# Linear attention mixed with an MLP: the head's loads rearranged, and W4's last 64 features of four chunks multiplied in row halves

## The chip, the cores and the metric

The kernel runs on one core of a Trainium2 chip. The metric is device time in microseconds (us) of one execution. Five engines work side by side, each with its own instruction stream: TensorE (PE in the profile; PEld is its weight loads) multiplies, VectorE (DVE) and ScalarE (ACT) do elementwise work and empty PSUM, GpSimd (POOL) does small setups, and SyncE (SP) mostly issues transfers (DMA). Transfers are also issued by ACT and POOL.

## The reference, cut to what matters

2048 rows of x with 640 features, 32 heads of 20, everything in bfloat16:

```
g = sigmoid((x * gate_w).sum(-1, keepdims=True))

# a: linear attention
q, k, v = split(x @ wqkv);  phi(t) = where(t > 0, t + 1, exp(t)) + 1e-6
num = phi(q) @ (phi(k)^T @ v);  den = phi(q) @ sum(phi(k))
a = (num / (den + 1e-6)) @ wo

# b: mixer and MLP
h  = gelu(layernorm(x) @ w1);  x1 = x + shift4(h) @ w2
b  = x1 + gelu(layernorm(x1) @ w3) @ w4        # w4 is 1728 x 640

out = g * a + (1 - g) * b
```

1728 features are 13 blocks of 128 and a rest of 64.

## The kernel before, in words

The rows are cut into 16 chunks of 128 (c), four of which make a tile of 512 (t). The order on each engine is that of the code; nothing is moved by a scheduler. PSUM is used as four pairs of banks: `pair()` returns the next free one, and a unit that takes a pair waits until the one that had it has been emptied.

The stages, in order: k for all 16 chunks (`k_mm`, L199; `k_evac` empties it), q (`q_unit`, L246), G = x^T phi(k) (`g_unit`, L347), w1 of the MLP (L377), the attention matrices (`kv_unit` L396, `m_unit` L415), w2 (L452), and then for each tile w3 (L499, its 64 rest features at L504) with the next tile's w2 and the attention output (L483) between, and w4 (`w4_unit`, L524).

The k stage multiplies x^T by wk. `wk_sb` has 640 columns of wk and one more, the gate vector, so that the right half of each product (321 columns) also gives x . gate_w. The matmul wants x transposed (`xT`). For chunks 0 to 2 x is loaded in rows and turned by TensorE into PSUM (`x_turn`, L215), from where DVE copies it (L216). For chunks 3 to 15 a transposing transfer brings it straight from memory (L124). wk comes in five pieces of 128 rows (`dc` 0 to 4), all issued by ACT (L129). The gate column is a POOL transfer that scatters 640 single values (L152). `warmup` (L210) multiplies zeros, to keep TensorE busy. The k matmuls of the first three chunks are interleaved by hand as their pieces land (L222 to L233); from chunk 3 on they go chunk by chunk.

SP's queue holds, in order: x chunks 0, 1, 2, the four transposing transfers, wq, the rest of x, and the other weights. wq is re-ordered by five POOL copies (L179) before q uses it. The transfers that SP and ACT issue use eight semaphores in turn, and an issue waits until the last transfer on its semaphore has landed.

In W4 each chunk has two halves of 320 output columns, each a sum over 14 matmuls: 13 blocks of 128 features, and one for the rest of 64. The rest's gelu output h2 holds chunks 0 and 1 on the upper 64 partitions and chunks 2 and 3 on the lower. So there are two copies of the rest's w4 rows, the other 64 partitions of which POOL sets to zero (L432, L433), and the fourteenth matmul runs over all 128 rows. DVE then computes the output chunk `oc` from PSUM (L530), and SP stores it. The last chunk goes in two halves (L526), each stored by itself.

Of the kernel before, what the change touches and what calls it, by code (L numbers as in the profile page):

```python
# [16 lines left out]
def kernel(  # L17
# [25 lines left out]
    FR = F - FF * P
# [12 lines left out]
    out2 = out.rearrange("b s d -> (b s) d")  # L56
# [27 lines left out]
    r_bf = const.tile([P, TS], BF16)  # L84
    ident = const.tile([P, P], BF16)
    ones32 = const.tile([P, 32], BF16)
    wz = const.tile([P, TS], BF16)
    mhalf = const.tile([P, CPT], F32)
    hmask = const.tile([P, H], F32)
    zbd = const.tile([P, DC, H], BF16)  # L90
# [5 lines left out]
    gate = const.tile([P, NCH], F32)  # L96
    omg = const.tile([P, NCH], F32)
# [20 lines left out]
    sp, aq, gq = nc.sync, nc.scalar, nc.gpsimd  # L118

    def load_x(c0, c1):  # L120
        sp.dma_start(x_sb[:, c0:c1, :], x2[c0 * P:c1 * P, :].rearrange("(c p) d -> p c d", p=P))

    def load_xT(c0, c1):
        sp.dma_start_transpose(xT[:, :, c0 * P:c1 * P], x2[c0 * P:c1 * P, :])  # L124

    NPE = 3
    load_x(0, 1)
    for dc in range(DC):
        aq.dma_start(wk_sb[:, dc, 0:D], A_wqkv[dc * P:(dc + 1) * P, D:2 * D])  # L129
    load_x(1, 2)  # L130
    load_x(2, 3)
    load_xT(3, 4)
    load_xT(4, 8)
    load_xT(8, 12)
    load_xT(12, 16)
    sp.dma_start(wq_raw, wqkv_v[:, :, 0:D])
    load_x(3, 8)
    load_x(8, 12)
    load_x(12, 16)
    sp.dma_start(wv_sb[:], wqkv_v[:, :, 2 * D:3 * D])  # L140
# [18 lines left out]
    nc.gpsimd.affine_select(out=hmask[:], in_=hmask[:], compare_op=ALU.is_ge, fill=0.0,
                            base=0, pattern=[[-4, H]], channel_multiplier=1)  # L160
# [25 lines left out]
    def phi(dst, src, n):  # L186
        e = e_p.tile([P, 1024], BF16, name="e")
        ev = e[:, 0:n]
        if len(src.shape) == 3:
            ev = ev.rearrange("p (h e) -> p h e", h=src.shape[1])  # L190
        nc.scalar.activation(ev, src, ACT.Exp)  # L191
        nc.vector.tensor_scalar(e[:, 0:n], e[:, 0:n], 1.0, 1e-6, op0=ALU.min, op1=ALU.add)  # L192
        nc.vector.scalar_tensor_tensor(dst, src, 0.0, ev, op0=ALU.max, op1=ALU.add)

    def k_mm(pt, c, dcs):
        for dc in dcs:
            for hf in range(2):
                n = HD + hf
                nc.tensor.matmul(pt[:, hf, 0:n], lhsT=xT[:, dc, c * P:(c + 1) * P],  # L199
                                 rhs=wk_sb[:, dc, hf * HD:hf * HD + n], start=(dc == 0), stop=(dc == DC - 1))  # L200

    def k_evac(pt, c):
        nc.scalar.copy(ylog[:, c:c + 1], pt[:, 1, HD:HD + 1])
        phi(pk[:, c, :].rearrange("p (h e) -> p h e", h=2), pt[:, :, 0:HD], D)

    warm = pair()

    def warmup(n, w=TS):
        for i in range(n):
            nc.tensor.matmul(warm[:, 1, 0:w], lhsT=wz[:, 0:P], rhs=wz[:, 0:w], start=True, stop=True)  # L210

    def x_turn(c):
        ptb = warm[:, 0, :].bitcast(BF16)
        for dc in range(DC):
            nc.tensor.transpose(ptb[:, dc * P:(dc + 1) * P], x_sb[:, c, dc * P:(dc + 1) * P], ident[:])  # L215
        nc.vector.tensor_copy(xT[:, :, c * P:(c + 1) * P], ptb[:, 0:D].rearrange("p (c s) -> p c s", c=DC))  # L216

    warmup(5)
    kp = [pair() for _ in range(3)]
    x_turn(0)  # L220
    warmup(5, P)
    k_mm(kp[0], 0, (0,))  # L222
    x_turn(1)
    k_mm(kp[0], 0, (1,))
    warmup(2, P)
    x_turn(2)
    k_mm(kp[1], 1, (0, 1))
    k_mm(kp[0], 0, (2,))
    k_mm(kp[1], 1, (2,))
    k_mm(kp[2], 2, (0, 1, 2))  # L230
    for dc in (3, 4):
        for c in range(3):
            k_mm(kp[c], c, (dc,))  # L233
    for c in range(3):
        k_evac(kp[c], c)
    for c in range(3, NCH):
# [191 lines left out]
        ln1_apply(3 * CPT + cc)  # L428
    s1.close()
    w4p = ctx.enter_context(tc.tile_pool(name="w4p", bufs=1))  # L430
    w4_sb = w4p.tile([P, FF + 2, D], BF16)
    nc.gpsimd.memset(w4_sb[FR:P, FF, :], 0.0)  # L432
    nc.gpsimd.memset(w4_sb[0:FR, FF + 1, :], 0.0)  # L433
    nc.gpsimd.dma_start(w4_sb[:, 0:FF, :], B_w4[0:FF * P, :].rearrange("(c p) f -> p c f", p=P))
    nc.gpsimd.dma_start(w4_sb[0:FR, FF, :], B_w4[FF * P:F, :])
    nc.gpsimd.dma_start(w4_sb[FR:P, FF + 1, :], B_w4[FF * P:F, :])
    h2p = ctx.enter_context(tc.tile_pool(name="h2p", bufs=1))
    x1p = ctx.enter_context(tc.tile_pool(name="x1p", bufs=8))
    st = {}
# [5 lines left out]
    def w2_unit(t, cc):  # L445
        c = t * CPT + cc
        if cc == 0:
            st[t] = dict(x1=[], mv=small.tile([P, CPT, 2], F32, name="mv2"))
        pt = pair()
        for hf in range(2):  # L450
            for fc in range(DC):
                nc.tensor.matmul(pt[:, hf, 0:HD], lhsT=hsT[:, fc, 2 + c * P:2 + (c + 1) * P],  # L452
                                 rhs=w2_sb[:, fc, hf * HD:(hf + 1) * HD], start=(fc == 0), stop=(fc == DC - 1))
        x1 = x1p.tile([P, D], F32, name="x1")
        nc.vector.tensor_tensor(x1[:].rearrange("p (h e) -> p h e", h=2), pt[:, :, 0:HD],  # L455
                                x_sb[:, c, :].rearrange("p (h e) -> p h e", h=2), op=ALU.add)
        ln_stats(st[t]["mv"][:, cc, :], x1[:], small.tile([P, 2, 6], F32, name="bnst")[:])
        st[t]["x1"].append(x1)
# [14 lines left out]
    def x1_scale(t, cc):  # L473
        c = t * CPT + cc
        x1 = st[t]["x1"][cc]
        nc.scalar.activation(x1[:], x1[:], ACT.Copy, scale=omg[:, c:c + 1])
# [30 lines left out]
        nc.scalar.activation(h2[:, 2 * i * TS:2 * i * TS + n], pt[:].rearrange("p h e -> p (h e)")[:, 0:n],  # L507
                             ACT.Gelu_apprx_tanh)

    def w4_unit(t, cc):  # L510
        c = t * CPT + cc
        h2, x1 = st[t]["h2"], st[t]["x1"][cc]
        last = c == NCH - 1
        oc = outp.tile([P, D], BF16, name="oc")
        pts = [pair(), pair()] if last else [pair()] * 2
        for hf in range(2):
            hs = slice(hf * HD, (hf + 1) * HD)
            for fc in range(FF + 1):
                if fc < FF:
                    w, l = w4_sb[:, fc, hs], h2[:, fc * TS + cc * P:fc * TS + (cc + 1) * P]  # L520
                else:
                    v, o = cc // 2, FF * TS + (cc % 2) * P
                    w, l = w4_sb[:, FF + v, hs], h2[:, o:o + P]
                nc.tensor.matmul(pts[hf][:, hf, 0:HD], lhsT=l, rhs=w, start=(fc == 0), stop=(fc == FF))  # L524
            if last:
                nc.vector.scalar_tensor_tensor(oc[:, hs], pts[hf][:, hf, 0:HD], omg[:, c:c + 1], x1[:, hs],  # L526
                                               op0=ALU.mult, op1=ALU.add)
                nc.sync.dma_start(out2[c * P:(c + 1) * P, hs], oc[:, hs])
        if not last:
# [21 lines left out]
    for t in range(NT):  # L551
        for i in range(NW3):
            w3_unit(t, i)
            if i < CPT and t + 1 < NT:
                w2_unit(t + 1, i)
            if 2 <= i < 2 + CPT:
                att_unit(t, i - 2)
        if t + 1 < NT:
            ln2_rstd(t + 1, 0, CPT)
            for cc in range(CPT):  # L560
                ln2_apply(t + 1, cc)
        for cc in range(CPT):
            if t + 1 < NT:
                x1_scale(t + 1, cc)
            w4_unit(t, cc)


# [28 lines left out]
```

## Time and profile before

| | us |
|---|---|
| median of 9 runs | 275.02 |
| lowest and highest | 274.70, 275.41 |
| profiled execution | 275.02 |
| its span, first to last instruction | 273.3 |
| TensorE busy | 264.5 (97%) |
| VectorE busy | 141.0 (52%) |
| ScalarE busy | 84.5 (31%) |
| GpSimd busy | 29.2 (11%) |

The span is what the engines' instructions cover; 1.7 us of the execution lie around it. A busy TensorE is not a TensorE at its peak, since matmuls overlap and each one's record lasts longer than its share of the time. Records of the form `L199 PE MATMUL out<-in` name the code line, the engine, the tile written and the tiles read.

### The profile page before, as it was taken

How to read it: one execution, taken by the hardware profiler on the slowest of the kernel's cores; microseconds unless marked ns; L12 is line 12 of the kernel's file. 1: busy time of each engine (PE TensorE's matmuls, PEld its weight loads, DVE VectorE, ACT ScalarE, POOL GpSimd, SP SyncE). 2: the span in 40 equal slices, each digit the busy share in tenths (PEclk: the TensorE clock that was granted, in tenths of full speed). 3: DMA queues.
4: the chain of work that ended last, by engine and by line, in shares of the span. 5: the costliest groups of instructions: out<-in, count | busy, mean ns of one | idle time of the engine just before them, and what ended most of it. 6: DMA issues, size and time to landing. Idle time of an engine off the chain costs nothing.

```text
span 273.3 us, 4333 instructions
## 1 busy us (share of the span) xinstructions
PE 264.5 (97%) x1764; PEld 161.0 (59%) x1781; DVE 141.0 (52%) x275; ACT 84.5 (31%) x124; POOL 29.2 (11%) x65
## 2 busy tenths in 40 slices
PE   5899999999999999999999999999999999999994
PEld 2567644456665564555577555577565577555673
DVE  1169865999994988556242256242256332112212
ACT  1065535531145715831250121250121250232100
POOL 7303100001227223000100000100000000000000
PEclk9999999999999999999999999999999999999999
DMA  7999984100474895000041100051100071100011
GB/s 176 229 240 369 337 269 173 26 2 0 82 110 99 266 170 95 3 0 2 0 94 53 48 0 2 0 100 46 48 2 0 1 93 53 48 2 0 0 50 48
DMA packets 41380, 22.82 MB, mean 83 GB/s; under 512 B 32080, under 2 KB 40272, under 8 KB 41360
## 3 DMA queue, kind: packets, MB, share of 16 engines
q1 hardware_dynamic: 40112, 19.42, 29.5%
q0 software_dynamic: 528, 2.30, 2.6%
q10 hardware_dynamic: 720, 0.82, 1.0%
q8 instruction: 14, 0.23, 0.4%
q14 instruction: 6, 0.05, 0.1%
HBM read 12.21 MB, written 2.62 MB: 54 GB/s over the span
## 4 chain that ended last, share of the span: by engine, by line
PE 94%; DMA 2%; ACT 1%; issue 1%; DVE 0%; ACTq 0%; POOLq 0%
PE pp L524 22%; PE pp L499 20%; PE pp L347 8%; PE pp L452 8%; PE pp L483 8%; PE pp L377 8%; PE pp L246 8%; PE pp L199 8%; DMA wk_sb<-in_gate_w_dram 2%; PE pp L415 1%; PE pp L504 1%; ACT e L191 1%; PE pp L262 0%; PE pp L285 0%; PE pp L215 0%
## 5 line engine op out<-in xcount | busy, mean ns | idle before, releaser
L524 PE MATMUL pp<-w_sb,h 128*128 128x320 bf16 x448 | 61.5, 299 | 0.0
L499 PE MATMUL pp<-lnxT,w_sb 128*128 128x512 bf16 x249 | 59.8, 379 | 0.6
L507 ACT ACTIVATE h<-pp 128x1024 bf16<-128x1024 f32 (+1 forms) x28 | 27.8, 993 | 103.8 <-PE pp L499 95.5
L524 PEld LDWEIGHTS <-h 128*128 128x128 bf16 x448 | 43.5, 98 | 17.5 <-issue 0.8
L499 PEld LDWEIGHTS <-w_sb 128*128 128x128 bf16 x260 | 25.4, 98 | 26.7
L530 DVE SCALAR_TENSOR_TENSOR oc<-pp,omg,x 128x640 bf16<-128x640 f32 x15 | 13.3, 884 | 44.7 <-PE pp L524 44.7
L486 DVE SCALAR_TENSOR_TENSOR x<-pp,gate,x 128x640 f32<-128x640 f32 x16 | 13.9, 868 | 29.4 <-PE pp L483 29.4
L199 PE MATMUL pp<-wk_sb,xT 128*128 128x320 bf16 (+1 forms) x160 | 24.8, 317 | 1.9 <-DMA wk_sb<-in_gate_w_dram 1.6
L455 DVE TENSOR_TENSOR x<-pp,x_sb 128x640 f32<-128x640 f32 x16 | 13.1, 820 | 23.4 <-PE pp L452 23.4
L483 PE MATMUL pp<-m_sb,pqT 128*128 128x320 bf16 x160 | 24.3, 299 | 0.0
L191 ACT ACTIVATE e<-pp 128x640 bf16<-128x640 f32 (+1 forms) x26 | 21.2, 830 | 9.3 <-PE pp L246 9.3
L452 PE MATMUL pp<-w_sb,hsT 128*128 128x320 bf16 x160 | 23.9, 299 | 0.0
L347 PE MATMUL pp<-pk,x_sb 128*128 128x320 bf16 x160 | 22.2, 299 | 0.0
L246 PE MATMUL pp<-xT,wq_sb 128*128 128x512 bf16 x97 | 21.8, 379 | 0.2
L199 PEld LDWEIGHTS <-xT 128*128 128x128 bf16 x160 | 16.4, 103 | 7.4 <-issue 0.6
L318 POOL TENSOR_SCALAR rstd<-mv 128x4 f32<-128x4 f32 (+1 forms) x11 | 3.5, 320 | 158.4 <-DVE mv L324 158.4
L452 PEld LDWEIGHTS <-hsT 128*128 128x128 bf16 x160 | 15.6, 98 | 8.2 <-issue 0.3
L483 PEld LDWEIGHTS <-pqT 128*128 128x128 bf16 x160 | 15.7, 98 | 7.7
L347 PEld LDWEIGHTS <-x_sb 128*128 128x128 bf16 x160 | 15.5, 98 | 6.7 <-issue 0.7
L377 PE MATMUL pp<-lnxT,w_sb 128*128 128x512 bf16 x77 | 17.8, 379 | 0.7 <-ACT hsT L381 0.5
L246 PEld LDWEIGHTS <-wq_sb 128*128 128x128 bf16 x100 | 9.7, 98 | 11.7 <-issue 0.3
L192 DVE TENSOR_SCALAR e<-e 128x640 bf16<-128x640 bf16 (+1 forms) x26 | 9.6, 368 | 9.1 <-ACT e L191 8.6
(84 smaller groups left out, 204.0 us busy)
## 6 DMA issues: line engine op xcount, KB each, us to landing
out_dram<-oc SPq DMA_DIRECT2D x15, 160.0 KB, 1.8
w_sb<-in_B_w_dram SPq DMA_DIRECT2D x1, 2160.0 KB, 9.4
w_sb<-in_B_w_dram POOLq DMA_DIRECT2D x1, 2080.0 KB, 10.8
x_sb<-in_A_x_dram SPq DMA_DIRECT2D x2, 640.0 KB, 10.0
wo_sb<-in_A_wo_dram SPq DMA_DIRECT2D x6, 160.0 KB, 7.6
wk_sb<-in_A_wqkv_dram ACTq DMA_DIRECT2D x5, 160.0 KB, 5.9
hsT<-in_A_wqkv_dram SPq DMA_DIRECT2D x1, 800.0 KB, 5.3
x_sb<-in_A_x_dram SPq DMA_DIRECT2D x1, 800.0 KB, 6.9
```

The lines of the kernel that those rows point to most:

```text
L191: nc.scalar.activation(ev, src, ACT.Exp)
L199: nc.tensor.matmul(pt[:, hf, 0:n], lhsT=xT[:, dc, c * P:(c + 1) * P], rhs=wk_sb[:, dc, hf * HD:hf * HD + n], start=(dc == 0), stop=(dc == ...
L246: nc.tensor.matmul(pt[:, t % 2, :], lhsT=wq_sb[:, dc, j * P:(j + 1) * P], rhs=xT[:, dc, t * TS:(t + 1) * TS], start=(dc == 0), stop=(dc == ...
L347: nc.tensor.matmul(pt[:, hf, 0:HD], lhsT=x_sb[:, c, fc * P:(fc + 1) * P], rhs=pk[:, c, hf * HD:(hf + 1) * HD], start=(c == 0), stop=(c == ...
L377: nc.tensor.matmul(pt[:, i, :], lhsT=w, rhs=lnxT[t][:, dc, :], start=(dc == 0), stop=(dc == DC - 1))
L452: nc.tensor.matmul(pt[:, hf, 0:HD], lhsT=hsT[:, fc, 2 + c * P:2 + (c + 1) * P], rhs=w2_sb[:, fc, hf * HD:(hf + 1) * HD], start=(fc == 0), ...
L483: nc.tensor.matmul(pt[:, hf, 0:HD], lhsT=pqT[:, j, c * P:(c + 1) * P], rhs=m_sb[:, j, hf * HD:(hf + 1) * HD], start=(j == 0), stop=(j == D ...
L486: nc.vector.scalar_tensor_tensor(x1, pt[:, :, 0:HD], gate[:, c:c + 1], x1, op0=ALU.mult, op1=ALU.add)
L499: nc.tensor.matmul(pt[:, k, :], lhsT=w3_sb[:, dc, fc * P:(fc + 1) * P], rhs=lnT[:, dc, :], start=(dc == 0), stop=(dc == DC - 1))
L507: nc.scalar.activation(h2[:, 2 * i * TS:2 * i * TS + n], pt[:].rearrange("p h e -> p (h e)")[:, 0:n], ACT.Gelu_apprx_tanh)
L524: nc.tensor.matmul(pts[hf][:, hf, 0:HD], lhsT=l, rhs=w, start=(fc == 0), stop=(fc == FF))
L530: nc.vector.scalar_tensor_tensor(oc[:].rearrange("p (h e) -> p h e", h=2), pts[0][:, :, 0:HD], omg[:, c:c + 1], x1[:].rearrange("p (h e) - ...
```

## The change

In the head, wk's pieces are issued by ACT (0, 2, 4) and SP (1, 3) in turn. The gate vector is loaded as five rows of 128 (`g5`), turned by TensorE, and copied by DVE into `wk_sb`'s last column. Only x chunk 0 is turned by TensorE, in two parts with a PSUM pair each; chunks 1 to 15 come by seven transposing transfers, chunks 1, 2 and 3 singly, 4 to 7 by twos, 8 to 15 by fours. Chunk 0's k matmuls go in the order 0, 2, 1, 4, 3 of the pieces, the left half first. The warm-up multiplies a constant of ones instead of a tile of zeros that DVE set.

In W4 the tile's four chunks are done together: chunks 0 and 2 first, 13 blocks each; then the rests of all four chunks (`w4_rest`), each over its own 64 partitions and not over 128; then chunks 1 and 3, 13 blocks each. The rest's sums end chunks 0 and 2 and begin chunks 1 and 3. The second copy of the rest's weights lies on the lower 64 partitions of the first, and the zeroing is gone. In the last tile, chunk 3's left half goes ahead of chunk 1, and its right half ends the kernel.

```diff
-    load_x(0, 1)
-    for dc in range(DC):
-        aq.dma_start(wk_sb[:, dc, 0:D], A_wqkv[dc * P:(dc + 1) * P, D:2 * D])
-    load_x(1, 2)
-    load_x(2, 3)
-    load_xT(3, 4)
-    load_xT(4, 8)
-    load_xT(8, 12)
-    load_xT(12, 16)
+    load_x(0, 1)
+    load_wk(aq, 0)
+    load_wk(aq, 2)
+    load_wk(sp, 1)
+    sp.dma_start(g5[:], gate_w.rearrange("(c p) -> c p", p=P))
+    load_wk(aq, 4)
+    load_wk(sp, 3)
+    for c0, c1 in ((1, 2), (2, 3), (3, 4), (4, 6), (6, 8), (8, 12), (12, 16)):
+        load_xT(c0, c1)
     sp.dma_start(wq_raw, wqkv_v[:, :, 0:D])
-    load_x(3, 8)
+    load_x(1, 8)
...
-    with nc.allow_non_contiguous_dma(reason="gate column"):
-        gq.dma_start(wk_sb[:, :, D:D + 1], gate_w.rearrange("(c p o) -> p c o", p=P, o=1))
...
+    warmup(6)
+    kp = pair()
+    turns = [(pair()[:, 0, :].bitcast(BF16), a, b) for a, b in ((0, 2), (2, DC))]
+    tg = warm[:, 0, :].bitcast(BF16)
+    for n, (ptb, a, b) in enumerate(turns):
+        for dc in range(a, b):
+            nc.tensor.transpose(ptb[:, (dc - a) * P:(dc - a + 1) * P], x_sb[:, 0, dc * P:(dc + 1) * P], ident[:])
+        nc.vector.tensor_copy(xT[:, a:b, 0:P], ptb[:, 0:(b - a) * P].rearrange("p (c s) -> p c s", c=b - a))
     warmup(2, P)
...
+    order = (0, 2, 1, 4, 3)
+    k_mm(kp, 0, order[:3], (0,), order[4])
+    nc.tensor.transpose(tg[:, 0:DC], g5[:], ident[0:DC, 0:DC])
+    nc.vector.tensor_copy(wk_sb[:, :, D], tg[:, 0:DC])
+    k_mm(kp, 0, order[3:4], (0,), order[4])
+    k_mm(kp, 0, order[:4], (1,), order[4])
+    k_mm(kp, 0, order[4:], last=order[4])
+    k_evac(kp, 0)
+    for c in range(1, NCH):
...
-    w4_sb = w4p.tile([P, FF + 2, D], BF16)
-    nc.gpsimd.memset(w4_sb[FR:P, FF, :], 0.0)
-    nc.gpsimd.memset(w4_sb[0:FR, FF + 1, :], 0.0)
+    w4_sb = w4p.tile([P, FF + 1, D], BF16)
...
+    def w4_rest(t, ptss, start):
+        for u in range(2):
+            for hf in range(2):
+                for v in range(2):
+                    rows = slice(FR * v, FR * (v + 1))
+                    pts = ptss[u + 2 * v]
+                    if pts is not None:
+                        nc.tensor.matmul(pts[hf][:, hf, 0:HD], lhsT=st[t]["h2"][rows, FF * TS + u * P:FF * TS + (u + 1) * P],
+                                         rhs=w4_sb[rows, FF, hf * HD:(hf + 1) * HD], start=u == 1, stop=u == 0)
...
+    def w4_tile(t):
+        last = t == NT - 1
+        pts = {cc: [pair()] * 2 for cc in (0, 2)}
+        for cc in (0, 2):
+            if t + 1 < NT:
+                x1_scale(t + 1, cc)
+            for hf in range(2):
+                w4_mm(t, cc, pts[cc], hf, True)
+        for cc in (1, 3):
+            pts[cc] = [pair()] * 2
+        w4_rest(t, pts, True)
+        for cc in (0, 2):
+            w4_out(t, cc, pts[cc], (0, 1))
+        for cc, hf in ((3, 0), (1, 0), (1, 1), (3, 1)) if last else ((1, 0), (1, 1), (3, 0), (3, 1)):
+            if t + 1 < NT and hf == 0:
+                x1_scale(t + 1, cc)
+            w4_mm(t, cc, pts[cc], hf, False)
+            if last and cc == 3:
+                w4_out(t, cc, pts[cc], (hf,))
+            elif hf == 1:
+                w4_out(t, cc, pts[cc], (0, 1))
```

What this moves shows at three places. The first is SP's queue at the start, before (DMAHW0 to 7 are the eight semaphores; the code lines are each kernel's own):

```order
L121 DMA x_sb<-in_A_x_dram 128x640 x3
L124 DMA_TRANSPOSE xT<-in_A_x_dram 128x5x128
L124 DMA_TRANSPOSE xT<-in_A_x_dram 128x5x512 [waits DMAHW1_49]
L124 DMA_TRANSPOSE xT<-in_A_x_dram 128x5x512 [waits DMAHW2_49]
L124 DMA_TRANSPOSE xT<-in_A_x_dram 128x5x512 [waits DMAHW3_49]
L136 DMA hsT<-in_A_wqkv_dram 128x5x640 [waits DMAHW4_49]
```

And now (`hsT` holds wq for a while, and `g` is `g5`):

```order
L121 DMA x_sb<-in_A_x_dram 128x640
L127 DMA wk_sb<-in_A_wqkv_dram 128x640
L133 DMA g_89<-in_gate_w_dram 5x128
L127 DMA wk_sb<-in_A_wqkv_dram 128x640
L124 DMA_TRANSPOSE xT<-in_A_x_dram 128x5x128
L124 DMA_TRANSPOSE xT<-in_A_x_dram 128x5x128 [waits DMAHW0_49]
L124 DMA_TRANSPOSE xT<-in_A_x_dram 128x5x128 [waits DMAHW1_49]
L124 DMA_TRANSPOSE xT<-in_A_x_dram 128x5x256 [waits DMAHW2_49]
L124 DMA_TRANSPOSE xT<-in_A_x_dram 128x5x256 [waits DMAHW3_49]
L124 DMA_TRANSPOSE xT<-in_A_x_dram 128x5x512 [waits DMAHW4_49]
L124 DMA_TRANSPOSE xT<-in_A_x_dram 128x5x512 [waits DMAHW5_49]
L138 DMA hsT<-in_A_wqkv_dram 128x5x640 [waits DMAHW6_49]
```

Three transposing transfers more stand ahead of wq, and two wk pieces and the gate ahead of the first of them.

The second place is TensorE at its first k matmuls, before (DMASW0 is the gate column's transfer):

```order
L210 MATMUL pp<-wz 128x128
L199 LDWEIGHTS xT
L199 MATMUL pp<-wk_sb,xT 128x320 [waits DMAHW0_49]
L199 LDWEIGHTS xT
L199 MATMUL pp<-wk_sb,xT 128x321 [waits DMASW0_49]
L215 LDWEIGHTS x_sb [waits DMAHW3_49]
L215 MATMUL pp<-ident,x_sb 128x128
```

And now:

```order
L198 LDWEIGHTS xT [waits DVE_49]
L198 MATMUL pp<-wk_sb,xT 128x320 [waits DMAHW2_49]
L198 LDWEIGHTS xT
L198 MATMUL pp<-wk_sb,xT 128x320 [waits DMAHW3_49]
L223 LDWEIGHTS g_89 [waits DMAHW5_49]
L223 MATMUL pp<-ident,g_89 128x5
L198 LDWEIGHTS xT
L198 MATMUL pp<-wk_sb,xT 128x320 [waits DMAHW4_49]
L198 LDWEIGHTS xT
L198 MATMUL pp<-wk_sb,xT 128x321 [waits DVE_49]
```

The second k matmul used to wait for the scattered column; now the gate's turn follows three left halves, and the first right half waits for DVE's copy of it.

The third place is TensorE in W4. Before, in the first tile, where one chunk ends and the next begins (the numbers tell the PSUM pairs apart):

```order
L524 LDWEIGHTS h2_1376
L524 MATMUL pp_1601<-w4_sb_1101,h2_1376 128x320
L524 LDWEIGHTS h2_1376
L524 MATMUL pp_1634<-w4_sb_1101,h2_1376 128x320 [waits PE_49]
L524 LDWEIGHTS h2_1376
L524 MATMUL pp_1634<-w4_sb_1101,h2_1376 128x320
```

And now, in the second tile, where chunk 2's blocks end and the rests run:

```order
L503 LDWEIGHTS h2_1718
L503 MATMUL pp_1942<-w4_sb_1090,h2_1718 128x320
L514 LDWEIGHTS h2_1718
L514 MATMUL pp_1941<-w4_sb_1090,h2_1718 128x320
L514 LDWEIGHTS h2_1718
L514 MATMUL pp_1942<-w4_sb_1090,h2_1718 128x320
L514 LDWEIGHTS h2_1718
L514 MATMUL pp_1941<-w4_sb_1090,h2_1718 128x320
L514 LDWEIGHTS h2_1718
L514 MATMUL pp_1942<-w4_sb_1090,h2_1718 128x320
L514 LDWEIGHTS h2_1718
L514 MATMUL pp_1997<-w4_sb_1090,h2_1718 128x320 [waits DVE_49]
```

One pair at a time was filled; now neighbouring matmuls go to two pairs by turns.

More of the change, by code (lines that the diff above doesn't have):

```diff
@@ L86 @@
     ones32 = const.tile([P, 32], BF16)
-    wz = const.tile([P, TS], BF16)
+    g5 = const.tile([DC, P], BF16)
     mhalf = const.tile([P, CPT], F32)
@@ L124, in load_xT, with load_wk @@
         sp.dma_start_transpose(xT[:, :, c0 * P:c1 * P], x2[c0 * P:c1 * P, :])
-    NPE = 3
+    def load_wk(q, dc):
+        q.dma_start(wk_sb[:, dc, 0:D], A_wqkv[dc * P:(dc + 1) * P, D:2 * D])
     load_x(0, 1)
-    for dc in range(DC):
-        aq.dma_start(wk_sb[:, dc, 0:D], A_wqkv[dc * P:(dc + 1) * P, D:2 * D])
-    load_x(1, 2)
-    load_x(2, 3)
-    load_xT(3, 4)
-    load_xT(4, 8)
-    load_xT(8, 12)
-    load_xT(12, 16)
+    load_wk(aq, 0)
[6 more added lines that the diff above has]
+        load_xT(c0, c1)
     sp.dma_start(wq_raw, wqkv_v[:, :, 0:D])
-    load_x(3, 8)
+    load_x(1, 8)
     load_x(8, 12)
@@ L147 @@
     sp.dma_start(w3_sb[:], B_w3.rearrange("(c p) f -> p c f", p=P))
-    nc.vector.memset(wz[:].bitcast(U32), 0)
-    with nc.allow_non_contiguous_dma(reason="gate column"):
-        gq.dma_start(wk_sb[:, :, D:D + 1], gate_w.rearrange("(c p o) -> p c o", p=P, o=1))
+    nc.gpsimd.memset(mhalf[:], -0.5)
     nc.gpsimd.memset(ident[:], 1.0)
@@ L156 @@
     nc.vector.memset(ones32[:], 1.0)
-    nc.gpsimd.memset(mhalf[:], -0.5)
     nc.gpsimd.memset(hmask[:], 1.0)
@@ L193, in phi, with k_mm @@
         nc.vector.scalar_tensor_tensor(dst, src, 0.0, ev, op0=ALU.max, op1=ALU.add)
-    def k_mm(pt, c, dcs):
+    def k_mm(pt, c, dcs, hfs=(0, 1), last=DC - 1):
         for dc in dcs:
-            for hf in range(2):
+            for hf in hfs:
                 n = HD + hf
                 nc.tensor.matmul(pt[:, hf, 0:n], lhsT=xT[:, dc, c * P:(c + 1) * P],
-                                 rhs=wk_sb[:, dc, hf * HD:hf * HD + n], start=(dc == 0), stop=(dc == DC - 1))
+                                 rhs=wk_sb[:, dc, hf * HD:hf * HD + n], start=(dc == 0), stop=(dc == last))
     def k_evac(pt, c):
@@ L206 @@
     warm = pair()
+    one = nc.const_aps.tensor(1.0, (P, TS), BF16)
     def warmup(n, w=TS):
         for i in range(n):
[L210 to L224, printed above, removed]
-    warmup(2, P)
[L226 to L236, printed above, removed]
+            nc.tensor.matmul(warm[:, 1, 0:w], lhsT=one[:, 0:P], rhs=one[:, 0:w], start=True, stop=True)
+    warmup(6)
[6 more added lines that the diff above has]
+        nc.vector.tensor_copy(xT[:, a:b, 0:P], ptb[:, 0:(b - a) * P].rearrange("p (c s) -> p c s", c=b - a))
+    warmup(2, P)
+    order = (0, 2, 1, 4, 3)
[7 more added lines that the diff above has]
+    for c in range(1, NCH):
         pt = pair()
@@ L430 @@
     w4p = ctx.enter_context(tc.tile_pool(name="w4p", bufs=1))
-    w4_sb = w4p.tile([P, FF + 2, D], BF16)
-    nc.gpsimd.memset(w4_sb[FR:P, FF, :], 0.0)
-    nc.gpsimd.memset(w4_sb[0:FR, FF + 1, :], 0.0)
+    w4_sb = w4p.tile([P, FF + 1, D], BF16)
     nc.gpsimd.dma_start(w4_sb[:, 0:FF, :], B_w4[0:FF * P, :].rearrange("(c p) f -> p c f", p=P))
     nc.gpsimd.dma_start(w4_sb[0:FR, FF, :], B_w4[FF * P:F, :])
-    nc.gpsimd.dma_start(w4_sb[FR:P, FF + 1, :], B_w4[FF * P:F, :])
+    nc.gpsimd.dma_start(w4_sb[FR:P, FF, :], B_w4[FF * P:F, :])
     h2p = ctx.enter_context(tc.tile_pool(name="h2p", bufs=1))
@@ L508, in w3_unit, with w4_mm, w4_out @@
                              ACT.Gelu_apprx_tanh)
-    def w4_unit(t, cc):
-        c = t * CPT + cc
[L512 to L529, printed above, removed]
+    def w4_mm(t, cc, pts, hf, start):
+        for fc in range(FF):
+            nc.tensor.matmul(pts[hf][:, hf, 0:HD], lhsT=st[t]["h2"][:, fc * TS + cc * P:fc * TS + (cc + 1) * P],
+                             rhs=w4_sb[:, fc, hf * HD:(hf + 1) * HD], start=start and fc == 0,
+                             stop=not start and fc == FF - 1)
+    def w4_rest(t, ptss, start):
[7 more added lines that the diff above has]
+                                         rhs=w4_sb[rows, FF, hf * HD:(hf + 1) * HD], start=u == 1, stop=u == 0)
+    def w4_out(t, cc, pts, hfs):
+        c = t * CPT + cc
+        x1 = st[t]["x1"][cc]
+        oc = oc_of.setdefault(c, None) or outp.tile([P, D], BF16, name="oc")
+        oc_of[c] = oc
+        if len(hfs) == 2:
             nc.vector.scalar_tensor_tensor(oc[:].rearrange("p (h e) -> p h e", h=2), pts[0][:, :, 0:HD],
@@ L533, in w4_unit @@
             nc.sync.dma_start(out2[c * P:(c + 1) * P, :], oc[:])
+        else:
+            hf = hfs[0]
+            hs = slice(hf * HD, (hf + 1) * HD)
+            nc.vector.scalar_tensor_tensor(oc[:, hs], pts[hf][:, hf, 0:HD], omg[:, c:c + 1], x1[:, hs],
+                                           op0=ALU.mult, op1=ALU.add)
+            nc.sync.dma_start(out2[c * P:(c + 1) * P, hs], oc[:, hs])
+    oc_of = {}
+    def w4_tile(t):
[19 more added lines that the diff above has]
+                w4_out(t, cc, pts[cc], (0, 1))
     for cc in range(CPT):
@@ L561 @@
                 ln2_apply(t + 1, cc)
[L562 to L565, printed above, removed]
+        w4_tile(t)
 _INS = ['A_x', 'A_wqkv', 'A_wo', 'B_x', 'B_w1', 'B_w2', 'B_w3', 'B_w4', 'gate_w']
```

## The prediction

> **What bounds the kernel now.** I read the page first, for which engine carries the span, then the chain that ended last, then the first 25 us in order of time with the landings of their transfers, since half of the change lies there.
>
> ```profile
> span 273.3 us, 4333 instructions
> PE 264.5 (97%) x1764; PEld 161.0 (59%) x1781; DVE 141.0 (52%) x275; ACT 84.5 (31%) x124; POOL 29.2 (11%) x65
> PE 94%; DMA 2%; ACT 1%; issue 1%; DVE 0%; ACTq 0%; POOLq 0%
> 1.32 6.25 DMA wk_sb<-in_gate_w_dram
> ...
> 9.15 0.37 PE pp L210 x2
> 9.53 0.53 PE pp L215 x5
> 10.06 4.57 PE pp L199 x22
> ...
> 16.86 16.51 PE pp L199 x120
> 33.37 0.22 PE pp L246
> ...
> 37.69 1.20 PE pp L262 x32
> ...
> 74.95 0.33 PE pp L297 x4
> ...
> 85.12 0.78 PE pp L396 x15
> ...
> 92.62 2.83 PE pp L415 x80
> ...
> 115.30 2.16 PE pp L499 x10
> ...
> 136.67 0.67 PE pp L504 x10
> 137.34 15.32 PE pp L524 x112
> ```
>
> Rows of the chain are start, length, what ran, how often. TensorE carries 94% of it, and from 33.37 us on it hardly waits. So a gain is either a TensorE stream made shorter, or the k stage (L199) ending before 33.37. The change does one of each: W4 is four streams like the 15.32 us row, and the head holds the one long wait, for the gate vector.
>
> The k stage has 160 matmuls (16 chunks of 10). The row at 16.86 gives 16.51/120 = 0.1376 us each, so 22.0 us would do; it ends at 33.37. The missing 11.4 us are a late start, waits, and a low pace: 22 matmuls took 4.57 us. Two stretches of L199 show the pace; in brackets stands how many records touch a stretch.
>
> ```profile
> 10.10:13.10 3.00, 3.00 (x13) 1.00 1.28 257
> 17.00:33.00 16.00, 16.00 (x119) 1.00 1.04 345
> L199 PE MATMUL pp<-wk_sb,xT x160: 296/300/475, 5.6 to 33.1; 128*128 128x320 bf16 x80, 128*128 128x321 bf16 x80
> ```
>
> The slowest record lasts 0.475 us, so 13 records touching 3.00 us start (3.00 + 0.475)/13 = 0.267 us apart, about half the later pace (the clock column reads 1.00 in both and does not show it). With n at the wide spacing among the 22, 0.267n + 0.1376(22 - n) = 4.57 gives n = 12: the pace doubles at about 13.2 us, 4.1 us after TensorE last began to work without a gap (9.15).
>
> **The head, step by step.** These rows are the head's first turn and TensorE's two waits after it, the issues, the landings (us from the issue's start), and POOL's group that copies wq.
>
> ```profile
> 3.79 0.71 PE L215 MATMUL pp<-ident,x_sb 128*128 128x128 bf16 x5 [0.23 <-DMA x_sb<-in_A_x_dram]
> 4.54 0.49 DVE L216 COPY xT<-pp 128x640 bf16<-128x640 bf16 x1 [3.31 <-PE pp L215]
> 5.09 0.69 PE L210 MATMUL pp<-wz 128*128 128x128 bf16 x5 [0.58 <-DVE xT L216]
> 7.61 0.43 PE L199 MATMUL pp<-wk_sb,xT 128*128 128x321 bf16 x1 [1.56 <-DMA wk_sb<-in_gate_w_dram]
> 0.80 1.34 SPq L121 DMA_DIRECT2D x_sb<-in_A_x_dram  x3
> 2.19 1.29 SPq L124 DMA_TRANSPOSE xT<-in_A_x_dram  x1
> 3.76 5.02 SPq L124 DMA_TRANSPOSE xT<-in_A_x_dram  x1
> 12.26 3.32 SPq L124 DMA_TRANSPOSE xT<-in_A_x_dram  x1
> 15.62 0.58 SPq L136 DMA_DIRECT2D hsT<-in_A_wqkv_dram  x1
> xT<-in_A_x_dram SPq DMA_TRANSPOSE x1, 6.4
> xT<-in_A_x_dram SPq DMA_TRANSPOSE x1, 8.3
> xT<-in_A_x_dram SPq DMA_TRANSPOSE x1, 5.3
> hsT<-in_A_wqkv_dram SPq DMA_DIRECT2D x1, 800.0 KB, 5.3
> L179 POOL COPY wq_sb<-hsT 128x320 uint32<-128x320 uint32 x5 | 2.3, 509 | 11.5 <-DMA hsT<-in_A_wqkv_dram 11.5
> wk_sb<-in_A_wqkv_dram ACTq DMA_DIRECT2D x1, 160.0 KB, 6.9
> 2.50:5.00 2.50, 1.77 (x8) 0.71 (x7) 0.46 (x1) 0.64 (x1) 2.03 (x11) 1.00 1.04 360
> 5.00:7.50 2.50, 0.96 (x6) 0.64 (x6) 0.04 (x1) 0.64 (x1) 2.07 (x8) 1.00 0.99 122
> ```
>
> The last column of a stretch is GB/s: 360 until 5.0 us, then 122 while the gate column (landing at 1.32 + 6.25 = 7.57) is under way. wk's last piece was issued at 3.99 and landed 6.9 later, at 10.9.
>
> *wk and x chunk 0.* The x chunk is still SP's first load, so its turn still starts at 3.79. Now x chunk 0 and five wk pieces, 6 x 160 KB, are all issued ahead of anything else: from 2.5 us at 360 GB/s they are through at 5.2, some 0.5 later in place. ACT's fifth issue, which stood back to 3.99, is gone, and so is the gate column; its five rows ride on SP between two pieces. Two turns (2 x 0.14) and the copy of 256 of 640 columns (0.2 to 0.3 of the 0.49) let the first k matmul start at 4.5. A 0.2 us wait for the second copy and 0.4 for the gate's turn and copy (DVE is idle there), and ten matmuls at 0.267, end chunk 0 at 7.6.
>
> *x chunk 1 by DMA transpose.* SP now issues four plain loads first, at 0.45 each (1.34/3), so the first transpose is issued from 2.6 to 3.9. The three landings are at 8.6, 12.1 and 17.6, which is 5.1, 3.3 and 2.0 after the end of their issue. So chunk 1 lands between 5.9 and 9.0. I take 7.5, nearest to the middle row: the 5.1 was spent in the stretch beside the gate column, which is gone. TensorE then goes on at 7.6 without a gap; at 9.0 it would stand for 1.4 us.
>
> *The later chunks.* One chunk's issue is 1.29 and four chunks' 3.32, thus 0.6 plus 0.68 a chunk. Seven issues for 15 chunks take 14.5 us with gaps and end at 17.5; chunks 8 to 11 end theirs at 14.1 and land at 16.1 to 17.4. The k stage needs chunk 8 eight chunks before its end, at 18.3 by the sum below. wq goes out behind them at 17.6, lands 5.3 later at 22.9, and POOL's five copies (0.5 each) end at 25.5, before it is wanted. x_sb, wv, w1 and w3 shift back by some 2 us too, behind stages that begin after 56 us.
>
> *The pace.* Work without a gap begins at 4.5, but for the gate's turn, so 5.6 at the latest if chunk 1 is in time. With the 4.1 us of above the pace doubles at 8.6 to 9.7; I take 9.7. Until then (9.7 - 4.5 - 0.6)/0.267 = 17 matmuls are done, and the other 143 take 19.7: the k stage ends at 29.4 instead of 33.4. **Gain 4.0 us**, and 4.7 with 8.6 (14 before it, end 28.7). What follows is chained to TensorE and moves up with it.
>
> The Trainium skill (TensorE: Matmul & The Clock Gate, Part 1: The HAM clock gate) says that the array gets half its clock until it has been busy for about one free-running window of 3.4 us. The trace agrees: the pace doubles 4.1 us after gapless work starts. Worked out from that page (an estimate), the doubling would come between one and two windows after the start, and a gap would put it off by a whole window; this is the first rival's mechanism.
>
> **W4, step by step.** Before, a tile has 4 chunks x 2 halves x 14 matmuls = 112 in 15.32 us, 0.137 each. The fourteenth multiplies 64 live rows and 64 zero rows. After, 104 full matmuls and 8 on 64 rows each, in pairs on the upper and lower rows with outputs in different pairs of banks. If a pair runs side by side, it costs one. The nearest rows say so: four 32-row matmuls of 512 columns (L297) took 0.33 us, where one full one of 512 takes 2.16/10 = 0.216. Blocks that split the columns do the same: L262 32 in 1.20 (eight fours at 0.1376 would be 1.10), L415 80 in 2.83 (2.75), L504 ten of 256 columns in 0.67 (five at 0.108: 0.54). Each such block pays 0.08 to 0.13 on top, whatever its length; I take 0.11. So 8 x 0.137 = 1.09 becomes 4 x 0.137 + 0.11 = 0.66: 0.43 saved a tile, **1.7 us in all four**. The bounds are 2.2 (no cost on top) and -0.4 (no overlap, 4 x 0.11 more). Weights can't bind: L396 loads a full 128x128 set for each 0.052 us matmul, and a pair needs two in 0.137.
>
> The Trainium skill (TensorEngine Tiling (Array Packing), Key Properties) has a rule against the change: going to another tiling mode drains the array. The 0.08 to 0.13 per block would be that, and it is in the sum.
>
> The rest costs nothing here. The evacuations of chunks 0 and 2 fall in the middle of a tile, where DVE only waits; all four PSUM pairs are held, but the next tile takes them in the same order, and chunk 3's alone comes free last, four units before it is wanted. POOL loses two memsets near 87 us, off the chain. The tail is again 320 columns on DVE and an 80 KB store; chunk 1's full store is issued ahead of it while thirteen matmuls (1.8 us) run, so I add nothing.
>
> **Sum.** The profiled execution took 275.02 us, 1.7 more than its span, and is the median itself. 275.02 - 4.0 - 1.7 = **269.3**.
>
> **Rivals.**
> 1. *The pace doubles late.* Chunk 1 lands at 9.0 or the gaps count against it; gapless work starts at 8.6, the pace doubles at 12.7. Then (12.7 - 4.5 - 1.6)/0.267 = 25 matmuls before it, end 31.3, gain 2.1: 271.2. For it speaks that the kernel before, with gaps of 0.58 and 1.56 us, stayed at the low pace to 13.2; against it, that chunk 1's price of 5.1 has a cause that is removed. 0.24.
> 2. *The transposes set the pace.* If all are issued at the 5.02/4 = 1.25 us a chunk of the second issue, chunks 8 to 11 end theirs at 16.4, land at 19.7, and 80 matmuls later it is 30.7: gain 2.7, time 270.6. For it: that issue stood while ordinary loads ran. Against it: the later ones took 3.3. 0.17.
> 3. *The W4 pairs don't overlap* and only pay the 0.11: 275.02 - 4.0 + 0.4 = 271.4. L297 speaks against it; no row has 64-row strips. 0.08.
> 4. *Slower:* each of the 32 half-row matmuls waits for the one before to leave the array, at the 0.299 us that one lasts from start to end:
>
> ```profile
> L524 PE MATMUL pp<-w_sb,h 128*128 128x320 bf16 x448 | 61.5, 299 | 0.0
> ```
>
> That adds 32 x (0.299 - 0.137) = 5.2, more than the head gives: 276.2. It decides once a half-row matmul costs over 0.26 us (0.137 + 4.0/32). L297's four in 0.33 speak against it. 0.04.
>
> **Chances and range.** My forecast 0.45, the rivals 0.24, 0.17, 0.08, 0.04; two of the first three together, near 273, 0.02. The forecast's own range is 268.1 (4.7 and 2.2) to 270.2. All cases but the slower one and the pairs of rivals lie from 268.1 to 271.4; with 0.4 for the spread of the runs shown (274.7 to 275.41) and for a half-way gap, 268.0 to 272.0. Below 0.2% (0.55 us) a measurement of this kernel can't be told from no change: faster 0.94, same 0.02, slower 0.04.
>
> **What would show it.** In the profile after: no wait for the gate; the first k matmul near 4.5 us, chunk 1's near 7.6 with no wait for xT longer than 0.5 us; the row of q's first matmul at 29.4; L199's pace doubling near 9.7. In W4: 104 + 8 matmuls in 14.9 us a tile, the eight in 0.66. I am wrong on the head if TensorE stands for xT or wq, and on W4 if a tile still takes 15.3.

## The result, and the profile after

The changed kernel takes 268.02 us (median of 10 runs, 267.68 to 269.5); the kernel before, run beside it, 275.01. The ratio is 0.9765, with a 95% interval of 0.9749 to 0.9781: 6.0 to 6.9 us less. The profiled execution took 269.46, so it is one of the longer ones. These are its page's first lines and its chain (start, length, what ran, how often):

```profile
span 267.8 us, 4300 instructions
PE 262.0 (98%) x1751; PEld 157.3 (59%) x1768; DVE 140.3 (52%) x274; ACT 84.9 (32%) x124; POOL 26.8 (10%) x62
PE 97%; DMA 1%; issue 1%; ACT 0%; DVE 0%; ACTq 0%
0.80 2.96 DMA x_sb<-in_A_x_dram
...
3.81 0.71 PE pp L218 x5
4.52 0.21 PE pp L210 x2
4.73 0.95 PE pp L198 x3
5.69 0.11 PE pp L223
5.80 23.50 PE pp L198 x157
29.30 0.22 PE pp L239
...
52.20 4.35 PE pp L340 x32
...
70.88 0.33 PE pp L290 x4
71.21 4.45 PE pp L340 x32
...
121.77 1.36 PE pp L443 x10
...
133.27 7.17 PE pp L503 x52
140.44 0.65 PE pp L514 x8
141.09 7.17 PE pp L503 x52
```

The wait for the gate is gone from the chain, and from 3.81 us on TensorE hardly stops. The k stage ends at 29.30 where it ended at 33.37: 4.07 us. A W4 tile takes 7.17 + 0.65 + 7.17 = 14.99 us where it took 15.32: 0.33, or 1.3 in four. Together that is 5.4 of the 5.5 us between the two spans. The k stage's pace in this trace, as records of L198 that touch each microsecond:

```profile
8.00:9.00 1.00, 1.00 (x6) 1.00 0.84 143
9.00:10.00 1.00, 1.00 (x6) 1.00 1.01 224
10.00:11.00 1.00, 1.00 (x9) 1.00 1.06 182
11.00:12.00 1.00, 1.00 (x10) 1.00 0.81 169
```

It doubles just before 10 us, where the prediction had 9.7. But the median lies 1.4 us under this execution, and no part of the trace pair accounts for that. The experiments were chosen for that gap, for the parts of the head, and for W4's missing 0.1 us a tile.

### The profile page after: what moved, and what is told of

Read it like the earlier page. It is cut to its first block, busy times and chain, and to the rows that moved or that the text cites. A ratio compares the mean times of both kernels' runs of the same rounds, so it can differ in the third digit from the quotient of the medians.

```text
span 267.8 us, 4300 instructions
## 1 busy us (share of the span) xinstructions
PE 262.0 (98%) x1751; PEld 157.3 (59%) x1768; DVE 140.3 (52%) x274; ACT 84.9 (32%) x124; POOL 26.8 (10%) x62
## 4 chain that ended last, share of the span: by engine, by line
PE 97%; DMA 1%; issue 1%; ACT 0%; DVE 0%; ACTq 0%
PE pp L503 21%; PE pp L490 21%; PE pp L198 9%; PE pp L340 8%; PE pp L443 8%; PE pp L474 8%; PE pp L370 8%; PE pp L239 8%; DMA x_sb<-in_A_x_dram 1%; PE pp L408 1%; PE pp L495 1%; PE pp L514 1%; PE pp L255 0%; PE pp L278 0%; PE pp L389 0%
## 5 line engine op out<-in xcount | busy, mean ns | idle before, releaser
L503 PE MATMUL pp<-w_sb,h 128*128 128x320 bf16 x416 | 57.9, 299 | 0.0
L503 PEld LDWEIGHTS <-h 128*128 128x128 bf16 x416 | 40.1, 98 | 17.0 <-issue 1.9
L477 DVE SCALAR_TENSOR_TENSOR x<-pp,gate,x 128x640 f32<-128x640 f32 x16 | 13.9, 868 | 29.4 <-PE pp L474 29.4
L198 PE MATMUL pp<-wk_sb,xT 128*128 128x320 bf16 (+1 forms) x160 | 24.7, 318 | 0.0
L443 PE MATMUL pp<-w_sb,hsT 128*128 128x320 bf16 x160 | 23.9, 299 | 0.0
L340 PE MATMUL pp<-pk,x_sb 128*128 128x320 bf16 x160 | 22.2, 299 | 0.0
L198 PEld LDWEIGHTS <-xT 128*128 128x128 bf16 x160 | 16.2, 103 | 7.7 <-DVE xT L219 0.3
L443 PEld LDWEIGHTS <-hsT 128*128 128x128 bf16 x160 | 15.6, 98 | 8.2 <-issue 0.3
L340 PEld LDWEIGHTS <-x_sb 128*128 128x128 bf16 x160 | 15.5, 98 | 6.7 <-issue 0.7
```

Of the source, the lines that this page charges most:

```text
L340: nc.tensor.matmul(pt[:, hf, 0:HD], lhsT=x_sb[:, c, fc * P:(fc + 1) * P], rhs=pk[:, c, hf * HD:(hf + 1) * HD], start=(c == 0), stop=(c == ...
L477: nc.vector.scalar_tensor_tensor(x1, pt[:, :, 0:HD], gate[:, c:c + 1], x1, op0=ALU.mult, op1=ALU.add)
L503: nc.tensor.matmul(pts[hf][:, hf, 0:HD], lhsT=st[t]["h2"][:, fc * TS + cc * P:fc * TS + (cc + 1) * P], rhs=w4_sb[:, fc, hf * HD:(hf + 1) * ...
```

## The experiments

Times are medians. Each group of four ran on a chip of its own, beside the kernel before: 274.61 for e1 to e4, 274.78 for e5 to e8, 274.87 for e9 to e12. Ratios are to it, with 95% intervals.

**Head and W4 apart.** e1 has all of the diff above W4 and none of it from there on; e2 the other way round.

> The head of the changed kernel with the W4 of the kernel before. If head and W4 add up, and W4 gives 1.3 us (4 x (15.32 - 14.99) of the two traces), this lies 1.3 above the changed kernel, near 269.3, and a W4 tile takes 15.3 us again. Rival: most of the 7.0 us between the medians is W4, and the head gives 4.1 or less: near 271.

> The head of the kernel before with the W4 of the changed kernel. If W4 gives 1.3 us, near 273.7, with 7.17 + 0.65 + 7.17 us a tile and the k stage ending near 33 us. Rival: W4 gives the 1.7 us of the prediction or more (273.3 or less).

e1: 269.41 us, ratio 0.9824 (0.9799 to 0.985), so the head gives 4.1 to 5.5. e2: 273.69 us, ratio 0.9963 (0.9947 to 0.9978), so W4 gives 0.6 to 1.5. The chain, of e1 and then of e2:

```profile
27.83 4.32 PE pp L239 x20
...
131.80 15.32 PE pp L517 x112
```

```profile
32.84 4.32 PE pp L246 x20
...
136.80 7.17 PE pp L510 x52
143.97 0.65 PE pp L521 x8
144.62 7.17 PE pp L510 x52
```

W4's 1.3 us hold, not the 1.7 of the prediction. And with the same head, e1's k stage ended at 27.83, 1.5 us earlier than in the changed kernel's trace. So the head's gain differs from run to run. The old head differs too: in e2's trace its k stage ends at 32.84, not at 33.37.

**W4's pairs.** e3 turns the loops of `w4_rest`, so that four matmuls on the upper rows stand ahead of four on the lower. e6 puts all eight on the upper rows (the rests of chunks 2 and 3 are thus wrong rows).

```diff
 e3:
-        for u in range(2):
-            for hf in range(2):
-                for v in range(2):
+        for v in range(2):
+            for u in range(2):
+                for hf in range(2):
 e6:
-                    rows = slice(FR * v, FR * (v + 1))
+                    rows = slice(0, FR)
```

> The changed kernel with w4_rest's loops turned: the four matmuls on the upper 64 rows first, then the four on the lower. If two of them only run side by side when neighbours lie on different rows, the eight take about 8 x 0.137 + 0.1 = 1.2 us and not 0.65, and the kernel is 4 x 0.5 = 2.1 us slower than the changed one, near 270.1. Rival: a 64-row matmul is short by itself (0.65/8 = 0.08): no change.

> The changed kernel with all eight rest matmuls of a tile on the upper 64 rows (the rests of chunks 2 and 3 are so taken from the wrong rows). If two overlap only where they lie on different rows, and the turned order of loops changed nothing because TensorE takes the other half's from behind in its queue, the eight now take 8 x 0.136 + 0.11 = 1.2 us, a tile 15.5. Rival: a 64-row matmul lasts half as long whatever its rows: 0.65 us as before.

e3: 267.99 us, ratio 0.9764 (0.9741 to 0.9787), no change. e6 (one execution): 271.96. The chain's rows, of e3 and then of e6:

```profile
138.60 0.66 PE pp L514 x8
```

```profile
140.67 1.19 PE pp L514 x8
```

My expectation for e3 was wrong. Its rival, that half a row count takes half the time, falls with e6: on one half the eight take 1.19 us, 0.135 each plus 0.11. So two run side by side only on different halves. In e3, started strictly in order, the fifth could begin only behind the first four, and eight would need 7 x 0.135 = 0.95 at the least; they took 0.66. TensorE started the lower half's matmuls ahead of upper ones that stand before them. The start times in e3's trace say the same: in its first tile the second of the eight starts 0.01 us after the first, and it is the one that waits for the lower rows' weights. The interleaving in the code isn't needed.

**The parts of the head.** Each undoes one part of the changed kernel. e5 drops the long warm-up, e7 scatters the gate column by POOL again, e9 issues all of wk on ACT, and e10 turns chunks 1 and 2 on TensorE.

```diff
 e5:
-    warmup(6)
+    warmup(1, P)
 e7:
-    sp.dma_start(g5[:], gate_w.rearrange("(c p) -> c p", p=P))
...
+    gq.dma_start(wk_sb[:, :, D:D + 1], gate_w.rearrange("(c p o) -> p c o", p=P, o=1))
...
-    nc.tensor.transpose(tg[:, 0:DC], g5[:], ident[0:DC, 0:DC])
-    nc.vector.tensor_copy(wk_sb[:, :, D], tg[:, 0:DC])
 e9:
-    load_wk(sp, 1)
+    load_wk(aq, 1)
...
-    load_wk(sp, 3)
+    load_wk(aq, 3)
 e10:
-    for c0, c1 in ((1, 2), (2, 3), (3, 4),
+    load_x(1, 2)
+    load_x(2, 3)
+    for c0, c1 in ((3, 4),
...
+    x_turn(1)
     k_mm(kp, 0, order[4:], last=order[4])
...
+        if c == 1:
+            x_turn(2)
```

> The changed kernel without the six long warm-up matmuls (one short one is left). TensorE's first work is then the turn at 3.8. If the pace doubles some 3.4 to 7 us after work without long gaps begins, it does so at 8 to 11.5 us here (3.6, 5.8 and 9.8 were seen with this head and the warm-up), and each us later costs half a us: median 269 to 270.5. Rival: the warm-up on constants does nothing, and the times are those of the changed kernel (267.7 to 269.5).

> The changed kernel with the gate column scattered by POOL again (no five rows, no turn of them). If the scatter holds up the other transfers, as in the stretch of 122 GB/s of the kernel before, wk's last pieces and x chunk 1 land after 7.5 us too, the first right half starts at 7.6 or later, and the kernel is 1.5 to 3 us slower than the changed one: 269.5 to 271. Rival: only the first right half waits, the rest is filled: under 0.8 us slower.

> The changed kernel with all five pieces of wk on ACT, as before, and only the gate's rows on SP. The fifth issue stands until wk's first piece has landed (4.0 us), as in the kernel before. If that was what made wk's last piece late there (10.9 us), chunk 0 now waits for it from 7.4 us on, and the kernel is 0.5 to 2 us slower than the changed one run beside it. Rival: the transposes, now issued 0.9 us earlier, pay for it: no change.

> The changed kernel with x chunks 1 and 2 loaded in rows and turned by TensorE again. If the head's gain is TensorE time freed for k matmuls, ten turns at 0.11 to 0.14 us and the waits for two copies (0.5 us each) come back: 1 to 2 us slower than the changed one. Rival: the turns fill time in which TensorE waits for transfers anyway: no change.

| | median, us | ratio | interval |
|---|---|---|---|
| e5, no warm-up | 269.16 | 0.9799 | 0.9776 to 0.9822 |
| e7, gate scattered | 268.97 | 0.9797 | 0.9772 to 0.9823 |
| e9, wk on one queue | 272.35 | 0.9913 | 0.9896 to 0.993 |
| e10, three chunks turned | 269.10 | 0.9793 | 0.9773 to 0.9813 |
| changed kernel | 268.02 | 0.9765 | 0.9749 to 0.9781 |

e9 is the part that matters: 4 us. The fourth piece from its issue to its landing, the fifth's time to landing, then TensorE's rows in order of time:

```profile
2.21 5.86 DMA wk_sb<-in_A_wqkv_dram
wk_sb<-in_A_wqkv_dram ACTq DMA_DIRECT2D x1, 160.0 KB, 5.0
6.17 0.43 PE L198 MATMUL pp<-wk_sb,xT 128*128 128x320 bf16 x1 [0.65 <-DMA wk_sb<-in_A_wqkv_dram]
8.11 1.23 PE L198 MATMUL pp<-wk_sb,xT 128*128 128x320 bf16 x4 [1.40 <-DMA wk_sb<-in_A_wqkv_dram]
12.00:13.00 1.00, 1.00 (x6) 1.00 1.45 114
13.00:14.00 1.00, 1.00 (x8) 1.00 0.55 50
14.00:15.00 1.00, 1.00 (x10) 1.00 1.28 290
```

TensorE waits 2.05 us for wk, and about as much again comes on top of it: with these gaps the pace doubles only after 13 us, and the k stage ends at 32.27. I had expected 0.5 to 2 us in all. The step I named was wrong too. The longer wait, 1.40 us, is for the fourth piece, which was issued in its turn at 2.21; the fifth, whose issue stood until 4.07, landed at 9.0, before its matmuls' turn. The edit also moves the first transposing transfer from 2.52 to 1.66 us, ahead of the last pieces. No run parts that from the one queue.

The other three cost about 1 us each, and their intervals all reach into that of the changed kernel, so none of these prices is sharp. In e7 the scatter landed 5.2 us after its issue, beside 366 and then 199 GB/s, and TensorE waited 0.5 us, for wk:

```profile
wk_sb<-in_gate_w_dram POOLq DMA_DIRECT2D x1, 1.2 KB, 5.2
2.50:5.00 2.50, 2.21 (x11) 0.92 (x9) 0.65 (x2) 0.99 (x1) 2.03 (x11) 1.00 1.02 366
5.00:7.50 2.50, 2.02 (x8) 0.94 (x8) 0.00 (x0) 0.00 (x0) 2.07 (x8) 1.00 1.21 199
PE pp L199 <- DMA wk_sb<-in_A_wqkv_dram: 0.5, 1, 0.5
```

The changed kernel moves 362 and 188 GB/s in these two stretches, and chunk 1 landed at 7.0 us here, 7.1 there. So the scatter didn't hold up the other transfers, and my expectation of 1.5 to 3 us was wrong. Its price before was that the second k matmul stood behind it. e10 cost what I expected, at the low end: in its trace the pace doubles by 6 us, but k ends at 29.00, 0.8 later than in an early trace of the changed kernel (e12, below).

**The pace.** e4 (and again e11) warms up with seven matmuls and not six, until x chunk 0 lands. e12 is the changed kernel once more.

```diff
-    warmup(6)
+    warmup(7)
```

> The changed kernel with seven warm-up matmuls in place of six, so that TensorE works until x chunk 0 lands (0.83 + 7 x 0.43 = 3.8). If the pace doubles after a stretch of about 3.4 us that has to be nearly without gaps, and whose start against the kernel differs from run to run, it doubles earlier in more of the runs: the median falls by 0.3 to 1 us and the upper group of times (269.3 to 269.5) gets rarer. Rival: the 0.25 us gap before the turn doesn't matter, and the later gaps or the turn itself do: the same times as the changed kernel, in the same two groups.

> The kernel with seven warm-up matmuls once more, beside the changed kernel on the same chip. If the longer warm-up lets the pace double at 3.5 to 6 us in nearly every run, no time lies over 269, and the median is at or under the changed kernel's. Rival: chance; one in four lies at 269.3 to 269.5 here too.

> The changed kernel itself once more. If the place of the doubling decides the time, its times again lie between 267.6 and 269.5, and this trace's own pair fits the others: half a us of time for each us by which the pace doubles later, between 5.8 us (267.7) and 9.8 us (269.5). Rival: the two groups of times come from somewhere else, and the trace's doubling and time don't fit.

e4: 268.18 us, ratio 0.9773 (0.9752 to 0.9794). e11: 268.63, ratio 0.9776 (0.9755 to 0.9797). e12: 268.18, ratio 0.9768 (0.9742 to 0.9793). Of 16 runs of the changed kernel 4 lie at 269.3 to 269.61 and 12 under 268.7; of the 9 with seven none lies over 268.93. So the longer warm-up may take away the late ones (9 runs don't prove it), but its median isn't better. The pace in e12's trace, the waits of its weight loads for x (us in total, times, longest), and the start of q:

```profile
5.00:6.00 1.00, 0.93 (x5) 1.00 1.20 196
6.00:7.00 1.00, 1.00 (x8) 1.00 0.90 167
7.00:8.00 1.00, 1.00 (x10) 1.00 1.22 131
PEld L198 <- DMA xT<-in_A_x_dram: 1.6, 4, 0.7
28.22 4.32 PE pp L239 x20
```

Here it doubles more than 4 us earlier than in the first trace, and now the transposing transfers are late. All traces with the changed head (e4, e5 and e11 differ from it in the warm-up alone):

| trace | the pace doubles | k stage ends | profiled execution |
|---|---|---|---|
| e1, old W4 | before 4.2 | 27.83 | 269.33 |
| e4, seven | before 4.3 | 27.93 | 268.10 |
| e12, changed | near 5 | 28.22 | 268.40 |
| e11, seven | near 5 | 28.07 | 268.23 |
| e3, loops turned | 5 to 6 | 27.47 | 267.68 |
| e5, no warm-up | near 9 | 28.91 | 269.07 |
| changed, first | 9 to 10 | 29.30 | 269.46 |
| e6, rests on one half | near 10 | 29.53 | 271.96 |

From e3 to the first trace the doubling moves by some 4 us and the end of k by 1.8, half of it, and e5 lies between them. But e12's own trace misses what I expected of it: it doubles before e3's and yet takes 268.40, not 267.7: TensorE waits for x there. Earlier than in e3 no trace gains more. e4's turn, at 0.45 us where the first trace has 0.71, shows the doubling before any k matmul ran; two waits took the place of the low pace:

```profile
3.82 0.45 PE L218 MATMUL pp<-ident,x_sb 128*128 128x128 bf16 x5
PE pp L198 <- DMA wk_sb<-in_A_wqkv_dram: 0.7, 1, 0.7
PEld L198 <- DMA xT<-in_A_x_dram: 0.5, 1, 0.5
```

**A try for more.** e8 puts the transposing transfers directly behind x chunk 0 on SP, and wk on ACT in three loads.

```diff
-    load_wk(aq, 0)
-    load_wk(aq, 2)
-    load_wk(sp, 1)
-    sp.dma_start(g5[:], gate_w.rearrange("(c p) -> c p", p=P))
-    load_wk(aq, 4)
-    load_wk(sp, 3)
+    load_wk2(aq, 0, 1)
+    load_wk2(aq, 1, 3)
+    aq.dma_start(g5[:], gate_w.rearrange("(c p) -> c p", p=P))
+    load_wk2(aq, 3, 5)
...
-    order = (0, 2, 1, 4, 3)
+    order = (0, 1, 2, 3, 4)
```

> The changed kernel with x's transposing transfers directly behind x chunk 0 on SP, and wk in three loads (one piece, two, two) and the gate's rows on ACT. The first transpose is issued at 1.25 us and not at 2.5. In the runs where the pace doubles at 3.6 to 5.8 us, TensorE waited 0.5 to 1.0 us for xT; if the issue sets that, the k stage ends at 26.8 to 27.3 there and the median falls by 0.3 to 0.7 us, to 267.3 to 267.7. Rival: the transposes take the transfer engines from wk, chunk 0 waits longer, and the time stays or rises by up to 1 us.

```profile
PE pp L199 <- DMA wk_sb<-in_A_wqkv_dram: 1.0, 1, 1.0
28.02 0.22 PE pp L240
```

270.1 us, ratio 0.9829 (0.9802 to 0.9856). It is slower, as the rival said, but by 2 us and not by up to 1. The trace shows 1.0 us of waiting for wk, which now has transposes beside it. But it is the trace of an execution of 268.36 us, in which the pace had doubled before the first k matmul. Four of the six took 270.05 to 270.64, and of those there is no trace; a gap that puts the doubling off, as in e9, would fit, but is not shown. No version here beats the changed kernel.

## Why the prediction was right, and where it was off

- *The time.* 268.02 against 269.3 and a range of 268.0 to 272.0: right, but only just, and that is partly luck, since five of the ten runs lie under 268.0. The range's own sum is off there: 268.1 less the 0.4 for the spread is 267.7. Two errors of opposite sign lie behind it, the head too small (4.0 for 4.1 to 5.5) and W4 too large (1.7 for 1.3).
- *The loads of the head.* The first k matmul near 4.5 (it was 4.6), chunk 0 and 1 without a gap between: right. Chunk 1's transfer:

```profile
2.52 1.30 SPq L124 DMA_TRANSPOSE xT<-in_A_x_dram  x1
xT<-in_A_x_dram SPq DMA_TRANSPOSE x1, 4.6
9.79 3.51 SPq L124 DMA_TRANSPOSE xT<-in_A_x_dram  x1
xT<-in_A_x_dram SPq DMA_TRANSPOSE x1, 6.0
```

  It landed at 7.1 (7.5 forecast), chunks 8 to 11 at 15.8 (16.1 to 17.4). But the reason I gave for chunk 1 being early, that the scattered column had held the others up, is what e7 contradicts. What brings the lateness back is e9, with wk's five pieces on ACT and neither the scatter nor more than one x load ahead:

```profile
1.66 16.18 SPq L124 DMA_TRANSPOSE xT<-in_A_x_dram  x7
xT<-in_A_x_dram SPq DMA_TRANSPOSE x1, 6.5
```

  Chunk 1 takes 6.5 us from issue to landing, as the first transposing transfer did before (6.4), and not 4.6. So the lateness goes with how wk is issued, and the 7.5 came out for a wrong reason. Why stays open: in e8 wk is on ACT too, in three loads, and the first transfer takes 4.3.
- *The pace: the term that was mis-sized.* "With the 4.1 us of above the pace doubles at 8.6 to 9.7" gave 4.0 us for the head. It held in two traces (29.30 in the first and 29.53 in e6, against 29.4), but in three others with this head and six warm-up matmuls (e1, e3, e12) it doubles by 6 us, and e1 puts the head at 4.1 to 5.5. I had counted from gapless k work and given the warm-up no credit. Without the warm-up that count comes out, near 9 in e5, and none of e5's four runs lies under 268.58; with it 11 of 16 do. So the warm-up has credit in most runs. The Trainium skill (TensorE: Matmul & The Clock Gate, Part 1: The HAM clock gate) says that the window runs freely against the kernel's start, so that the same kernel changes over at different places in different runs; the traces agree (before 6, or near 10), but no run shows that the window is the reason. I quoted its one to two windows but started them at the k work alone.
- *W4: 0.33 a tile, not 0.43.* The eight took 0.65 (0.66 forecast). The failed step is "Each such block pays 0.08 to 0.13 on top", counted once. The 52 behind the block take 7.17 where the pace of L443 (1.36/10) gives 7.07: the way back costs 0.1 as well. The rows show it without W4: 32 matmuls of L340 take 4.35, and 4.45 right after the strips of r_unit at 70.88. I had both rows' like in the kernel before and didn't compare them:

```profile
56.26 4.35 PE pp L347 x32
...
75.28 4.45 PE pp L347 x32
```

  The Trainium skill (TensorEngine Tiling (Array Packing), Key Properties) has the rule that a change of mode drains the array; that fits a price in both directions.
- *The rivals.* 1 (late pace) has its place, but around an earlier centre. 2 (the transposes set the pace) is in part true of the runs that double early: in e12 TensorE stands for xT up to 0.7 us at a time, which I had named as a sign that the head is wrong. The waits for wk and x stop the head at 27.5 to 28.2. 3 and 4 fall with e6 and the 0.65.

## What to carry to other kernels

In the first microseconds ask what a late transfer does to TensorE's pace and not only how long it makes it wait: a gap of 2 us cost 4 here, since the doubling came later. Count work in strips with two changes of tiling, about 0.1 us each; eight half-row matmuls that take the time of four save 0.33 and not 0.54 us. And ask of a late transfer which piece TensorE stood for: in e9 it was the fourth, issued in its turn, and not the fifth, whose issue stood until the first had landed. Last, a trace of one run tells little where runs fall into groups: the first trace here was one of the 4 late ones in 16.

## What the runs showed that was not expected

- Matmuls on two row halves run side by side even where four of one half stand ahead of four of the other (0.66 us; 1.19 on one half). The Trainium skill (TensorE: Matmul & The Clock Gate, Part 3: Packing small matmuls — row/col tiling) says that matmuls start and end strictly in program order; the 0.66 us speak against it for this block.
- A transfer of 640 scattered values cost its neighbours next to nothing (e7).
- With the same six warm-up matmuls the pace doubles before the first k matmul in one run (e1) and after 9 us in another (the first trace). Each us of delay costs about half a us.
